# A linear-attention block with a gated FFN: one tile's mean on VectorE, one tile transposed by a DMA, and the last store from another queue

## The chip, the cores and the metric

The kernel runs on one core of a Trainium2 chip. The metric is the device time of one execution in microseconds; the kernel before has a median of 222.75 us over three runs (222.39 to 224.24).

## The reference

The input x has 2048 tokens of 640 features. All weights are bf16. Cut to what matters:

```python
xn = (x - mean(x)) / sqrt(var(x) + 1e-5)          # per token, no affine part
q, k, v = split(xn @ wqkv)                        # 32 heads of 20 features
phi = lambda t: where(t > 0, t + 1, exp(t)) + 1e-6
kv  = einsum("bhsd,bhse->bhde", phi(k), v)
z   = einsum("bhsd->bhd", phi(k))
o   = einsum("bhqd,bhde->bhqe", phi(q), kv) / (einsum("bhqd,bhd->bhq", phi(q), z) + 1e-6)
s   = o @ wo                                      # 640 to 640
g   = silu(relu(xn @ w1) @ w2)                    # FFN with 1728 inner features
out = x + s * g
```

## The kernel before

The tokens are 16 tiles of 128 and four chunks of 512. Every operation is put on an engine by hand, in the order in which the program text calls it; a small scheduler (`Sched`) finds the data dependences and adds the semaphore waits. So on each engine, and on each DMA queue, work runs strictly in the written order. Almost all DMAs are issued by SyncE's queue (SP); the first part of w1 is issued by ScalarE's.

The products with xn need it with features on partitions: `xnT`. Tiles 4 to 15 are normalised whole on VectorE (`LN_stats`: two statistics instructions, one aggregate, and 1/sqrt(var + eps) on GpSimd; then `LN_norm`) and transposed by a DMA from SP (`xnT_dma`, line 451). Tiles 0 to 3, which are needed first, are only centred (`center`, line 429) and their scale is applied later, when their keys and their gate are evicted. They are transposed by TensorE (`T_pe`, line 435, five 128 x 128 blocks) and copied out of PSUM by `T_copy` (lines 442 and 445). The mean of tiles 0 and 1 comes from `LN_stats` (lines 397 and 399); that of tiles 2 and 3 from an accumulating copy on ScalarE (`T_mean`, line 421).

While the inputs arrive, TensorE computes the first five of the 13 blocks of the FFN's inner features for chunk 0, one tile at a time: `H_first(t, fs, ks)` multiplies w1's blocks `fs`, contraction parts `ks`, with tile t (line 543, 128 columns each) into PSUM banks 2 to 6, and for tile 3 evicts each finished bank on ScalarE (`H_ev`, line 550). Bank 7 or 1 receives the transposes. The head of the program in its order:

```python
    H_first(0, (0, 1, 2), (0, 1)); H_first(0, (0, 1, 2), (2, 3, 4))   # two lines in the kernel
    LN_stats(1); center(1, 0, 2); T_pe(1, 0, 2, 7)
    ...
    H_first(0, (3, 4)); T_mean(3); center(2, 0, C)
    H_first(1, (0, 1)); T_pe(2, 0, C, 7); T_copy("ACT", 2, 0, C, 7); center(3, 0, C)
    H_first(1, (2, 3, 4)); T_pe(3, 0, C, 1); T_copy("ACT", 3, 0, C, 1)
    LN_stats(2); LN_stats(3)
    H_first(2); H_first(3, (4, 0, 1, 2, 3))
```

Then follow the keys of tiles 0 to 7 in turn with the rest of the FFN's blocks of chunk 0 (the list `order`): `K_step(t)` has the products of one tile's keys (`K_mm`, line 460, banks 0 and 1 or 6 and 7 by turns), the exponential on ScalarE (line 478 or 481), the rectified part (`K_relu`, line 487 on VectorE for tiles 0 and 1), and LayerNorm steps of tiles 4 to 7, whose transposes SP issues. The later chunks run queries (line 528) and FFN blocks by turns. After that come the sum over tokens of xn against phi(k) (line 786), the small products that make kv and kv times wo, the FFN's second half (line 841, `U_main`) with its silu on ScalarE, and the output products (line 887, `s_tile`): VectorE multiplies the gate in (line 909), adds x (line 894), and SP stores the tile (line 897). The last tile is cut in three parts (line 902): 320, 192 and 128 columns. GpSimd adds x to the first, VectorE to the other two together, and each of these two halves has its own store.

Of the kernel before, what the change touches and what calls it, by code (L numbers as in the profile page):

```python
# [4 lines left out]
ALU = mybir.AluOpType  # L5
ACTF = mybir.ActivationFunctionType
# [14 lines left out]
class Sched:  # L21
# [67 lines left out]

    def _hazards(self, R, W):  # L90
        agents = []
        for key in R:
            st = self.res.get(key)
# [29 lines left out]

    def op(self, E, fn, R=(), W=(), extra=()):
        return self.group(E, [fn], R, W, extra)
# [86 lines left out]
def bass_recurrent_scan__linear_attn_block__dense_activation_relu__prompt_kernel(  # L212
# [9 lines left out]
    Bb, S, D = A_x.shape  # L222
# [7 lines left out]
    C = D // P  # L230
# [3 lines left out]
    HN = D // 2  # L234
# [11 lines left out]
    out2 = out[0]  # L246
# [5 lines left out]
    xnT = reg1[:, :].rearrange("p (c s) -> p c s", c=C)  # L252
# [4 lines left out]
    xn = reg2[:, :].rearrange("p (t n) -> p t n", t=T)  # L257
# [6 lines left out]
    outb = reg3[:, VC * D:(VC + NOUT) * D].rearrange("p (a n) -> p a n", a=NOUT)  # L264
# [22 lines left out]
    xin = reg7[:, :].rearrange("p (t n) -> p t n", t=XR)  # L287
# [4 lines left out]
    ek = nc.alloc_sbuf_tensor("ek", [P, NEK, 2, D], bf)  # L292
# [27 lines left out]
    sc = Sched(nc, NDS)  # L320
    nds = [0]

    def dma(E, fn, R=(), W=(), extra=()):
        i = nds[0]
        nds[0] += 1
        return sc.dma(E, fn, i, R=R, W=W, extra=extra)

    def tok(t):
        return slice(P * t, P * (t + 1))
# [8 lines left out]
    def w_load(dst, src, key, extra=()):  # L338
# [9 lines left out]
          R=[("ident",)], W=[("ident",)])  # L348
# [16 lines left out]
    def w1_part(f):  # L365
# [6 lines left out]
        extra=[began])  # L372
# [21 lines left out]
    def LN_stats(t):  # L394
        xv = xin[:, t % XR, :]
        for a in range(2):
            sc.op("DVE", lambda eng, a=a: eng.bn_stats(stats[:, t, a, :], xv[:, HN * a:HN * (a + 1)]),  # L397
                  R=[("xin", t % XR)], W=[("stats", t, a)])
        sc.op("DVE", lambda eng: eng.bn_aggr(mv[:, t, :], stats[:, t, :, :].rearrange("p a b -> p (a b)")),
              R=[("stats", t, 0), ("stats", t, 1)], W=[("mv", t)])  # L400
        sc.op("POOL", lambda eng: eng.tensor_scalar(out=rsv[:, t:t + 1], in0=mv[:, t, 1:2], scalar1=EPS_LN,
                                                    scalar2=None, op0=ALU.add), R=[("mv", t)], W=[("rsv", t)])
        sc.op("POOL", lambda eng: eng.tensor_tensor(out=rsy[:, t:t + 1], in0=rsv[:, t:t + 1], in1=mhalf[:, :],
                                                    op=ALU.pow), R=[("rsv", t), ("mhalf",)], W=[("rsy", t)])
# [3 lines left out]
    def xnk(t, cs=range(C)):  # L408
        return [("xn", t, c) for c in cs]
# [7 lines left out]

    def T_mean(t):  # L420
        sc.op("ACT", lambda eng: eng.activation(out=ek[:, 0, 0, :], in_=xin[:, t, :], func=ACTF.Copy, scale=1.0 / D,
                                                accum_out=mean[:, t:t + 1]),
              R=[("xin", t)], W=[("mean", t), ("ek_e", 0)])

    sc.allow_unread.add(("ek_e", 0))

    def center(t, c0, c1):
        mk, m = (("mv", t), mv[:, t, 0:1]) if t < 2 else (("mean", t), mean[:, t:t + 1])
        return sc.op("DVE", lambda eng: eng.tensor_scalar(
            out=xn[:, t, P * c0:P * c1], in0=xin[:, t, P * c0:P * c1], scalar1=m, scalar2=None,  # L430
            op0=ALU.subtract), R=[("xin", t), mk], W=xnk(t, range(c0, c1)))

    def T_pe(t, c0, c1, b):
        psb = ps[b].bitcast(bf)
        sc.group("PE", [(lambda eng, c=c: eng.transpose(psb[:, P * c:P * (c + 1)], xn[:, t, P * c:P * (c + 1)], ident[:]))  # L435
                        for c in range(c0, c1)], R=xnk(t, range(c0, c1)) + [("ident",)], W=[("ps", b)])

    def T_copy(E, t, c0, c1, b):
        out = xnT[:, c0:c1, tok(t)]
        src = ps[b].bitcast(bf)[:, P * c0:P * c1].rearrange("p (c q) -> p c q", c=c1 - c0)  # L440
        if E == "ACT":
            sc.op("ACT", lambda eng: eng.activation(out=out, in_=src, func=ACTF.Copy), R=[("ps", b)],  # L442
                  W=xtk(t, range(c0, c1)))
        else:
            sc.op("DVE", lambda eng: eng.tensor_copy(out, src), R=[("ps", b)], W=xtk(t, range(c0, c1)))

    def xtk(t, cs=range(C)):
        return [("xnT", t, c) for c in cs]

    def xnT_dma(t):  # L450
        dma("SP", lambda eng: eng.dma_start_transpose(xnT[:, :, tok(t)], xn[:, t, :]), R=xnk(t), W=xtk(t))


    lastK = [None]
# [121 lines left out]
    def H_first(t, fs=range(5), ks=range(C)):  # L576
        for f in fs:
            H_mm(0, f, HF[f], P * t, P * t + P, ks)
            if t == 3:
                H_ev(0, f, HF[f])  # L580
# [10 lines left out]
    fill(1, 384)  # L591
    H_first(0, (0, 1, 2), (0, 1))
    H_first(0, (0, 1, 2), (2, 3, 4))
    LN_stats(1)
    center(1, 0, 2)
    T_pe(1, 0, 2, 7)
    held = center(1, 2, 5)
# [11 lines left out]
    H_first(0, (3, 4))  # L609
    T_mean(3)  # L610
    center(2, 0, C)
    H_first(1, (0, 1))
    T_pe(2, 0, C, 7)
    T_copy("ACT", 2, 0, C, 7)
    center(3, 0, C)
    H_first(1, (2, 3, 4))
    T_pe(3, 0, C, 1)
    T_copy("ACT", 3, 0, C, 1)
    LN_stats(2)
    LN_stats(3)  # L620
    H_first(2)
    H_first(3, (4, 0, 1, 2, 3))

    def z_split():
        sc.op("POOL", lambda eng: eng.tensor_copy(zhl[:, 0, :], zacc[:, :]), R=[("zacc",)], W=[("zhi",)])
        sc.op("POOL", lambda eng: eng.tensor_tensor(out=zhl[:, 1, :], in0=zacc[:, :], in1=zhl[:, 0, :], op=ALU.subtract),
# [54 lines left out]
            if t == 7:  # L681
                K_fin(t)

    order = [("K", 0), ("K", 1), 5, ("K", 2), 6, ("K", 3), 7, 8, ("K", 4), 9, ("K", 5), 10, ("K", 6), 11, ("K", 7), 12]
    for a in order:
        if isinstance(a, tuple):
            K_step(a[1])
        else:
            H_block(0, a, (2, 3, 4, 5)[(a - 5) % 4])
        if a == 6:  # L690
            LN_stats(6)
            K_fin(1)
            LN_norm(6)
            xnT_dma(6)
        if a == 8:
            LN_stats(7)
            K_fin(2)
            LN_norm(7)
            xnT_dma(7)
            K_fin(3)  # L700
# [4 lines left out]
    for j in range(1, J):  # L705
# [11 lines left out]
        for n, (kind, jj, f) in enumerate(blocks):  # L717
# [4 lines left out]
            if j + 1 < J:  # L722
# [6 lines left out]
                if n in (9, 12, 14, 17):  # L729
                    t = t0 + (9, 12, 14, 17).index(n)  # L730
# [27 lines left out]
    for a in range(2):  # L758
# [3 lines left out]
            W=[("w2", a)], extra=[lastX])  # L762
    for u in range(2):
        dma("SP", lambda eng, u=u: eng.dma_start(w2l[64 * u:64 * (u + 1), :], B_w2[NF * P:FF, :]),
            W=[("w2l", u)], extra=[lastX])
# [4 lines left out]
    for c in range(C):  # L770
        dma("SP", lambda eng, c=c: eng.dma_start(rep[:, c, :], rscr[P * c:P * (c + 1), :]),
            R=[("rscr", i) for i in range(J)], W=[("rep", c)], extra=[lastX])
# [61 lines left out]
    def bank(p, u):  # L834
        return 4 * ((p + 1) % 2) + 2 * u
# [43 lines left out]
    def s_tile(p, u, b, last=False):  # L879
        t = pairs[p][u]  # L880
        os_ = so[0] % NOUT
        so[0] += 1
        i = t // 4

        parts = [(b, 0, HN), (b + 1, HN, 512), (bank(7, 0), 512, D)] if last else [(b, 0, HN), (b + 1, HN, D)]
        for pb, lo, hi in parts:
            sc.group("PE", [(lambda eng, c=c, pb=pb, lo=lo, hi=hi: eng.matmul(  # L887
                ps[pb][:, 0:hi - lo], lhsT=pqT[:, c, tok(t)], rhs=wf[:, c, lo:hi],
                start=(c == 0), stop=(c == C - 1))) for c in range(C)],
                R=[("pqT", i, c) for c in range(C)] + wfk, W=[("ps", pb)])  # L890
        gk = [("g", t, 0), ("g", t, 1)]

        def add(E, lo, hi, keys):
            sc.op(E, lambda eng: eng.tensor_tensor(out=outb[:, os_, lo:hi], in0=tmpo[:, os_, lo:hi],  # L894
                                                   in1=xre[:, t, lo:hi], op=ALU.add),
                  R=[("tmpo", os_, k) for k in keys] + [("xre", t // 4)], W=[("outb", os_, k) for k in keys])
            dma("SP", lambda eng: eng.dma_start(out2[tok(t), lo:hi], outb[:, os_, lo:hi]),
                R=[("outb", os_, k) for k in keys])

        if last:  # L900
            for k, (pb, lo, hi) in enumerate(parts):
                sc.op("DVE", lambda eng, pb=pb, lo=lo, hi=hi: eng.tensor_tensor(  # L902
                    out=tmpo[:, os_, lo:hi], in0=ps[pb][:, 0:hi - lo], in1=g_sb[:, t, lo:hi], op=ALU.mult),
                    R=[("ps", pb)] + gk, W=[("tmpo", os_, k)])
                if k == 0:
                    add("POOL", lo, hi, (0,))
            add("DVE", HN, D, (1, 2))
        else:
            sc.op("DVE", lambda eng: eng.tensor_tensor(  # L909
                out=two(tmpo[:, os_, :]), in0=ps2(b, HN), in1=two(g_sb[:, t, :]), op=ALU.mult),  # L910
                R=[("ps", b), ("ps", b + 1)] + gk, W=[("tmpo", os_, k) for k in range(3)])
            add("DVE", 0, D, (0, 1, 2))
# [88 lines left out]
```

## Time and profile before

| | |
|---|---|
| median of three runs | 222.75 us (222.39 to 224.24) |
| profiled execution | 222.63 us, span 220.8 us |
| mean granted clock of TensorE | 0.998 |
| TensorE busy | 215.1 us of the span |
| VectorE, ScalarE, GpSimd busy | 113.4, 87.8, 43.8 us |
| DMA | 24.51 MB, mean 111 GB/s |

The span goes from the first to the last instruction that the profiler recorded. In a timeline row stand the start in us from the span's start, the duration, the engine (a q behind it is its sequencer, which issues DMAs), the line, the operation, the tile written and the tiles read by the program's names, shapes, and in brackets the idle time of the engine ahead of it and what ended it. `reg` is any of the large shared SBUF regions, `psT` is PSUM. Rows of one line that follow each other are merged and counted (x5). A DMA's landing is counted from its issue.

### The profile page before, as it was taken

To read this page: it belongs to the slowest core of one execution; us is meant where nothing else is said; L and a number is where in the kernel's file an instruction comes from. 1 tells how busy PE (TensorE), PEld (TensorE's weight loads), DVE (VectorE), ACT (ScalarE), POOL (GpSimd) and SP (SyncE) were. 2 spreads that over 40 slices of the span, in tenths; PEclk is the share of its full clock that TensorE was granted. 3 is DMA by queue.
4 is the path that set the end of the run, shared out by engine and by line. 5 is a ranking of instruction groups with operands and counts; after the bars stand their busy time and mean duration, and the time that the engine had idled before them with its cause. 6 is when DMAs were issued, how large, how long until landed. Compare 5 with 4: busy or idle time off the path is not lost.

```text
span 220.8 us, 3565 instructions
## 1 busy us (share of the span) xinstructions
PE 215.1 (97%) x1479; PEld 134.1 (61%) x1490; DVE 113.4 (51%) x193; ACT 87.8 (40%) x143; POOL 43.8 (20%) x66
## 2 busy tenths in 40 slices
PE   8899999999999999999999999999999999999994
PEld 2875554455545554444467778767767776776673
DVE  2848856789686999987700006603322222314063
ACT  3677775557656666555321114641021102110300
POOL 4232201269122997700000000000000000000001
PEclk9999999999999999999999999999999999999999
DMA  6994593213012105800069968378110100000002
GB/s 175 361 371 121 130 184 107 59 36 27 0 30 59 33 1 117 168 3 0 0 199 364 270 190 344 94 224 284 60 62 0 61 33 30 31 33 30 30 30 88
DMA packets 28812, 24.51 MB, mean 111 GB/s; under 512 B 11812, under 2 KB 28156, under 8 KB 28796
## 3 DMA queue, kind: packets, MB, share of 16 engines
q1 hardware_dynamic: 28140, 23.79, 37.3%
q10 hardware_dynamic: 656, 0.49, 0.9%
q8 instruction: 11, 0.18, 0.3%
q14 instruction: 5, 0.04, 0.1%
HBM read 15.75 MB, written 5.24 MB: 95 GB/s over the span
## 4 chain that ended last, share of the span: by engine, by line
PE 95%; DMA 2%; DVE 1%; issue 0%; SPq 0%
PE psT L841 26%; PE psT L543 25%; PE psT L786 10%; PE psT L460 10%; PE psT L528 10%; PE psT L887 10%; DMA reg<-in_A_x_dram 2%; PE psT L857 1%; PE psT L565 1%; PE psT L797 1%; PE psT L808 1%; PE psT L644 1%; PE psT L435 1%; DVE reg L902 0%; DVE stats L397 0%
## 5 line engine op out<-in xcount | busy, mean ns | idle before, releaser
L543 PE MATMUL psT<-reg 128*128 128x512 bf16 (+1 forms) x326 | 60.1, 330 | 1.3 <-DMA reg<-in_B_w_dram 0.7
L841 PE MATMUL psT<-reg,hT 128*128 128x320 bf16 x416 | 60.1, 299 | 0.0
L841 PEld LDWEIGHTS psT<-reg,hT 128*128 128x128 bf16 x416 | 40.4, 98 | 16.4 <-issue 1.1
L543 PEld LDWEIGHTS psT<-reg 128*128 128x128 bf16 x335 | 28.5, 98 | 26.6 <-ACT reg L442 1.0
L909 DVE TENSOR_TENSOR reg<-psT,reg 128x640 bf16<-128x640 f32 x15 | 12.4, 825 | 54.0 <-PE psT L887 54.0
L550 ACT ACTIVATE hT<-psT 128x512 bf16<-128x512 f32 x52 | 30.7, 599 | 16.1 <-PE psT L543 16.0
L875 ACT ACTIVATE reg<-psT 128x640 bf16<-128x640 f32 (+1 forms) x13 | 8.4, 661 | 44.3 <-PE psT L841 24.9
L894 POOL TENSOR_TENSOR reg<-reg 128x320 bf16<-128x320 bf16 x1 | 0.8, 787 | 124.6 <-DVE reg L902 124.6
L528 PE MATMUL psT<-reg 128*128 128x512 bf16 x98 | 24.4, 379 | 0.1
L460 PE MATMUL psT<-reg 128*128 128x320 bf16 x160 | 24.2, 299 | 0.0
L469 POOL TENSOR_TENSOR zacc<-zacc,reg 128x640 f32<-128x640 f32 x16 | 23.8, 1484 | 1.9 <-DVE reg L503 1.0
L887 PE MATMUL psT<-reg,pqT 128*128 128x320 bf16 (+2 forms) x165 | 24.0, 295 | 0.0
L786 PE MATMUL psT<-reg 128*128 128x320 bf16 x160 | 21.9, 299 | 0.0
L460 PEld LDWEIGHTS psT<-reg 128*128 128x128 bf16 x160 | 15.5, 98 | 8.3 <-ACT ek L481 0.3
L887 PEld LDWEIGHTS psT<-reg,pqT 128*128 128x128 bf16 x165 | 15.9, 98 | 6.0
L786 PEld LDWEIGHTS psT<-reg 128*128 128x128 bf16 x160 | 15.7, 98 | 6.2
L538 DVE SCALAR_TENSOR_TENSOR pqT<-er 128x512 bf16<-128x512 bf16 x20 | 17.1, 854 | 0.7
L528 PEld LDWEIGHTS psT<-reg 128*128 128x128 bf16 x100 | 9.7, 98 | 11.7 <-DVE er L536 0.6
L397 DVE BATCH_NORM_STATS2 stats<-reg 128x6 f32<-128x320 bf16 x32 | 14.0, 480 | 5.0 <-DMA reg<-in_A_x_dram 5.0
L535 ACT ACTIVATE er<-psT 128x512 bf16<-128x512 f32 x20 | 12.0, 598 | 8.9 <-PE psT L528 8.1
L536 DVE TENSOR_SCALAR er<-psT 128x512 bf16<-128x512 f32 x20 | 13.6, 679 | 3.0 <-ACT er L535 3.0
L503 DVE TENSOR_TENSOR reg<-ek 128x640 bf16<-128x640 bf16 x16 | 13.5, 844 | 1.5 <-ACT ek L494 1.0
(62 smaller groups left out, 133.3 us busy)
## 6 DMA issues: line engine op xcount, KB each, us to landing
reg<-in_A_x_dram SPq DMA_DIRECT2D x16, 160.0 KB, 3.5
rscr<-rden SPq DMA_DIRECT2D x4, 640.0 KB, 10.8
reg<-rscr SPq DMA_DIRECT2D x5, 512.0 KB, 6.2
reg<-in_A_x_dram SPq DMA_DIRECT2D x4, 640.0 KB, 6.9
out_dram<-reg SPq DMA_DIRECT2D x15, 160.0 KB, 1.8
reg<-in_A_wqkv_dram SPq DMA_DIRECT2D x2, 800.0 KB, 6.7
reg<-in_B_w_dram SPq DMA_DIRECT2D x1, 1120.0 KB, 5.6
reg<-in_B_w_dram SPq DMA_DIRECT2D x1, 960.0 KB, 9.3
```

The source lines that it names most:

```text
L397: sc.op("DVE", lambda eng, a=a: eng.bn_stats(stats[:, t, a, :], xv[:, HN * a:HN * (a + 1)]), R=[("xin", t % XR)], W=[("stats", t, a)])
L460: fns.append(lambda eng, a=a, k=k: eng.matmul(ps[b + a][:, 0:HN], lhsT=xnT[:, k, tok(t)], rhs=wqk[:, k, D + HN * a:D + HN * (a + 1)], star ...
L469: sc.op("POOL", lambda eng: eng.tensor_tensor(out=zacc[:, :], in0=zacc[:, :], in1=pk[:, t, :], op=ALU.add), R=[("zacc",), ("pk", t)], W=[( ...
L503: sc.op("DVE", lambda eng: eng.tensor_tensor(out=pk[:, t, :], in0=e_, in1=r_, op=ALU.add), R=[("ek_e", es), ("ek_r", es)], W=[("pk", t)])
L528: sc.group("PE", [(lambda eng, k=k: eng.matmul(ps[b], lhsT=wqk[:, k, P * f:P * (f + 1)], rhs=rhs(k), start=(k == 0), stop=(k == C - 1))) f ...
L536: sc.op("DVE", lambda eng: eng.tensor_scalar(out=r_, in0=ps[b], scalar1=0.0, scalar2=1e-6, op0=ALU.max, op1=ALU.add), R=[("ps", b), ("er_e ...
L538: sc.op("DVE", lambda eng: eng.scalar_tensor_tensor(out=pqT[:, f, schunk(j)], in0=e_, scalar=1.0, in1=r_, op0=ALU.min, op1=ALU.add), R=[(" ...
L543: return sc.group("PE", [(lambda eng, k=k: eng.matmul(ps[b][:, lo:hi], lhsT=w1_sb[:, k, P * f:P * (f + 1)], rhs=xnT[:, k, 512 * j + lo:512 ...
L550: sc.op("ACT", lambda eng: eng.activation(out=hT[:, f, schunk(j)], in_=ps[b], func=ACTF.Relu), R=[("ps", b)], W=[("hT", j, f)])
L786: fns.append(lambda eng, t=t, a=a: eng.matmul(ps[b + a][:, 0:HN], lhsT=xn[:, t, P * k:P * (k + 1)], rhs=pk[:, t, HN * a:HN * (a + 1)], sta ...
L841: sc.group("PE", [(lambda eng, f=f, n=n: eng.matmul(ps[b + n][:, 0:HN], lhsT=hT[:, f, tok(t)], rhs=w2_sb[:, f, HN * n:HN * (n + 1)], start ...
L887: sc.group("PE", [(lambda eng, c=c, pb=pb, lo=lo, hi=hi: eng.matmul(ps[pb][:, 0:hi - lo], lhsT=pqT[:, c, tok(t)], rhs=wf[:, c, lo:hi], sta ...
```

## The change

Four edits. The mean of tile 1 is made by one VectorE tensor_scalar with an accumulated output, and `LN_stats(1)`, still needed for the variance, moves behind tile 3's DMA. Tile 3 is transposed by a DMA that ScalarE's queue issues, instead of by TensorE and a ScalarE copy; every later `xnT_dma` on SP waits until it has landed (`extra=first_T`). In TensorE's order six of tile 1's products move ahead of tile 2's transposes, and all of tile 3's blocks move behind the keys of tile 0. In the last tile the parts become 256, 192 and 192 columns; GpSimd adds the first 256, VectorE the other 384, and that second store is issued by ScalarE's queue.

```diff
+    def T_mean(t, E="ACT"):
+        if E == "ACT":
...
+        else:
+            sc.op("DVE", lambda eng: eng.tensor_scalar(out=ek[:, 1, 0, :], in0=xin[:, t, :], scalar1=1.0 / D, scalar2=0.0,
+                                                       op0=ALU.mult, op1=ALU.add, accum_out=mean[:, t:t + 1]),
+                  R=[("xin", t)], W=[("mean", t), ("ek_e", 1)])
...
-        mk, m = (("mv", t), mv[:, t, 0:1]) if t < 2 else (("mean", t), mean[:, t:t + 1])
+        mk, m = (("mv", t), mv[:, t, 0:1]) if t < 1 else (("mean", t), mean[:, t:t + 1])
...
-    def xnT_dma(t):
-        dma("SP", lambda eng: eng.dma_start_transpose(xnT[:, :, tok(t)], xn[:, t, :]), R=xnk(t), W=xtk(t))
+    first_T = []
+
+    def xnT_dma(t, E="SP"):
+        d = dma(E, lambda eng: eng.dma_start_transpose(xnT[:, :, tok(t)], xn[:, t, :]), R=xnk(t), W=xtk(t), extra=first_T)
+        if E != "SP":
+            first_T.append(d)
...
-    LN_stats(1)
+    T_mean(1, "DVE")
     center(1, 0, 2)
...
     center(2, 0, C)
-    H_first(1, (0, 1))
+    H_first(1, (0, 1, 2, 3, 4), (0, 1))
+    H_first(1, (0, 1), (2, 3, 4))
     T_pe(2, 0, C, 7)
     T_copy("ACT", 2, 0, C, 7)
     center(3, 0, C)
-    H_first(1, (2, 3, 4))
-    T_pe(3, 0, C, 1)
-    T_copy("ACT", 3, 0, C, 1)
+    H_first(1, (2, 3, 4), (2, 3, 4))
+    xnT_dma(3, "ACT")
+    LN_stats(1)
     LN_stats(2)
     LN_stats(3)
     H_first(2)
-    H_first(3, (4, 0, 1, 2, 3))
...
-    order = [("K", 0), ("K", 1), 5, ...]
+    order = [("K", 0), None, ("K", 1), 5, ...]        # None: H_first(3, (4, 0, 1, 2, 3))
...
-        parts = [(b, 0, HN), (b + 1, HN, 512), (bank(7, 0), 512, D)] if last else [(b, 0, HN), (b + 1, HN, D)]
+        parts = [(b, 0, 256), (b + 1, 256, 448), (bank(7, 0), 448, D)] if last else [(b, 0, HN), (b + 1, HN, D)]
...
-            add("DVE", HN, D, (1, 2))
+            add("DVE", 256, D, (1, 2), "ACT")
```

More of the change, by code (lines that the diff above doesn't have):

```diff
@@ L416, in LN_norm @@
             x_load(t + XR)
[L420 to L425, printed above, removed]
+    def T_mean(t, E="ACT"):
+        if E == "ACT":
+            sc.op("ACT", lambda eng: eng.activation(out=ek[:, 0, 0, :], in_=xin[:, t, :], func=ACTF.Copy, scale=1.0 / D,
+                                                    accum_out=mean[:, t:t + 1]),
+                  R=[("xin", t)], W=[("mean", t), ("ek_e", 0)])
+        else:
+            sc.op("DVE", lambda eng: eng.tensor_scalar(out=ek[:, 1, 0, :], in0=xin[:, t, :], scalar1=1.0 / D, scalar2=0.0,
+                                                       op0=ALU.mult, op1=ALU.add, accum_out=mean[:, t:t + 1]),
+                  R=[("xin", t)], W=[("mean", t), ("ek_e", 1)])
+    sc.allow_unread.update([("ek_e", 0), ("ek_e", 1)])
     def center(t, c0, c1):
-        mk, m = (("mv", t), mv[:, t, 0:1]) if t < 2 else (("mean", t), mean[:, t:t + 1])
+        mk, m = (("mv", t), mv[:, t, 0:1]) if t < 1 else (("mean", t), mean[:, t:t + 1])
         return sc.op("DVE", lambda eng: eng.tensor_scalar(
@@ L682, in K_step @@
                 K_fin(t)
-    order = [("K", 0), ("K", 1), 5, ("K", 2), 6, ("K", 3), 7, 8, ("K", 4), 9, ("K", 5), 10, ("K", 6), 11, ("K", 7), 12]
+    order = [("K", 0), None, ("K", 1), 5, ("K", 2), 6, ("K", 3), 7, 8, ("K", 4), 9, ("K", 5), 10, ("K", 6), 11, ("K", 7), 12]
     for a in order:
-        if isinstance(a, tuple):
+        if a is None:
+            H_first(3, (4, 0, 1, 2, 3))
+        elif isinstance(a, tuple):
             K_step(a[1])
@@ L891, in s_tile, with add @@
         gk = [("g", t, 0), ("g", t, 1)]
-        def add(E, lo, hi, keys):
+        def add(E, lo, hi, keys, Q="SP"):
             sc.op(E, lambda eng: eng.tensor_tensor(out=outb[:, os_, lo:hi], in0=tmpo[:, os_, lo:hi],
@@ L896, in add @@
                   R=[("tmpo", os_, k) for k in keys] + [("xre", t // 4)], W=[("outb", os_, k) for k in keys])
-            dma("SP", lambda eng: eng.dma_start(out2[tok(t), lo:hi], outb[:, os_, lo:hi]),
+            dma(Q, lambda eng: eng.dma_start(out2[tok(t), lo:hi], outb[:, os_, lo:hi]),
                 R=[("outb", os_, k) for k in keys])
```

## The prediction

> **What bounds the kernel now.** I read the parts of the page first: busy time, slices, and the chain that ended last.
>
> ```profile
> span 220.8 us, 3565 instructions
> PE 215.1 (97%) x1479; PEld 134.1 (61%) x1490; DVE 113.4 (51%) x193; ACT 87.8 (40%) x143; POOL 43.8 (20%) x66
> PE 95%; DMA 2%; DVE 1%; issue 0%; SPq 0%
> ```
>
> TensorE is busy for 97% of the span and carries 95% of the chain. The chain in order of time shows it without a gap from the second transposes to the last output product; the two rows at its end are VectorE's. Only the first 7 us and the last 4 us can be shortened by waiting less. In between, five transposes are all that the change takes off TensorE, so what matters is whether a new wait opens in the head. Next I read the head engine by engine in the timeline (start, duration, engine, line, tiles, count, what ended the idle time).
>
> ```profile
> 6.06 1.00 PE L543 MATMUL psT<-reg 128*128 128x128 bf16 x15 [0.72 <-DMA reg<-in_B_w_dram]
> 7.21 0.57 PE L435 MATMUL psT<-ident,reg 128*128 128x128 bf16 x5 [0.15 <-DVE reg L429]
> 7.62 1.35 PE L543 MATMUL psT<-reg 128*128 128x128 bf16 x20
> 8.81 0.44 PE L435 MATMUL psT<-ident,reg 128*128 128x128 bf16 x5
> 9.09 1.00 PE L543 MATMUL psT<-reg 128*128 128x128 bf16 x15
> 9.93 0.44 PE L435 MATMUL psT<-ident,reg 128*128 128x128 bf16 x5
> 10.20 2.96 PE L543 MATMUL psT<-reg 128*128 128x128 bf16 x50
> 13.00 2.88 PE L460 MATMUL psT<-reg 128*128 128x320 bf16 x20
> ```
>
> These rows are tile 0's blocks, tile 1's transposes, then by turns blocks and the transposes of tiles 2 and 3; from 10.20 the blocks of tiles 2 and 3, 50 products in 2.80 us, so 56 ns each; at 13.00 the keys of tiles 0 and 1. The chain gives those 20 key products 2.72 us, 1.36 per tile, so the keys are through at 15.72. This is my checkpoint: behind it the order on TensorE is the old one.
>
> ```profile
> 13.16 2.72 PE psT L460 x20
> ```
>
> **Part 1: tile 1's mean by accumulation.** Removed ahead of the centring are two statistics and one aggregate; added is one 640-wide tensor_scalar with an accumulated output, from the same arrival at 5.71.
>
> ```profile
> 5.71 0.89 DVE L397 BATCH_NORM_STATS2 stats<-reg 128x6 f32<-128x320 bf16 x2 [0.92 <-DMA reg<-in_A_x_dram]
> 6.63 0.21 DVE L399 BATCH_NORM_AGGREGATE mv<-stats 128x2 f32<-128x12 f32 x1
> 6.87 0.52 DVE L429 TENSOR_SCALAR reg<-reg,mv 128x256 bf16<-128x256 bf16 x2
> 8.10 0.38 DVE L429 TENSOR_SCALAR reg<-reg,mean 128x640 bf16<-128x640 bf16 x1
> 8.53 0.18 ACT L421 ACTIVATION_READ_ACCUMULATOR ek<-reg 128x1 f32 x1
> 15.38 0.89 DVE L487 TENSOR_SCALAR ek<-psT,rsy 128x640 bf16<-128x640 f32 x1 [2.08 <-ACT ek L478]
> 2.25 0.43 SPq L339 DMA_DIRECT2D reg<-in_B_w_dram  x1
> reg<-in_B_w_dram SPq DMA_DIRECT2D x1, 320.0 KB, 5.1
> ```
>
> No row shows a VectorE accumulation. Its bounds are a 640-wide tensor_scalar from SBUF (0.38) and one from PSUM (0.89), with up to 0.18 for reading the sum as ScalarE does. The mean is then ready between 6.09 and 6.78 instead of 6.84, and the centring starts 0.1 to 0.75 us earlier. TensorE cannot use that: its 15 products end at 6.06 + 15 x 0.056 = 6.90, so the transposes come at most 0.31 earlier, and behind them stand blocks 3 and 4 of tile 0, which need the second part of w1: issued 2.25, landed 5.1 later, at 7.35. With the tenth of a microsecond from a landing to its product they start at 7.45 instead of 7.62. The gain is 0.17 at most, 0 at least; I take 0.17. Tile 1's statistics, moved behind tile 3's centring, are wanted by its exponential at 16: five microseconds of cover.
>
> **Part 2: tile 3 off TensorE, and the new order.** From 7.45 TensorE has 26 products (10 of tile 0, 16 of tile 1) ahead of tile 2's transposes, which so start at 7.45 + 1.46 = 8.91, against 8.81. What follows waits for the copy out of PSUM.
>
> ```profile
> 9.29 0.70 ACT L442 ACTIVATE reg<-psT 128x640 bf16<-128x640 bf16 x1 [0.57 <-PE psT L435]
> 8.75 0.39 DVE L429 TENSOR_SCALAR reg<-reg,mean 128x640 bf16<-128x640 bf16 x1 [0.28 <-ACT ek L421]
> 12.08 2.56 ACT L550 ACTIVATE hT<-psT 128x512 bf16<-128x512 f32 x5 [0.97 <-PE psT L543]
> 14.55 0.79 ACT L478 ACTIVATE ek<-psT,rsy 128x640 bf16<-128x640 f32 x1
> ```
>
> In the old order copy 2 ends at 9.99, 1.18 after the first of its transposes, and 15 products and tile 3's five transposes (0.28) cover it up to 10.20. In the new order only nine products stand there (0.50): TensorE is free at 8.91 + 0.28 + 0.50 = 9.69, the copy is there at 8.91 + 1.18 = 10.09, and tile 2's blocks start at 10.12. So the five transposes saved turn into 0.43 of idling, and of all that only 0.08 is left. Then 25 products (1.40) and tile 0's keys (1.36) end at 12.88. The key weights are there in time, at 4.82 + 5.2 = 10.02:
>
> ```profile
> 4.82 0.38 SPq L339 DMA_DIRECT2D reg<-in_A_wqkv_dram  x1
> DMA to landing us min/median/max: 5.2/5.2/5.2
> ```
>
> **The transfer decides.** At 12.88 TensorE wants tile 3. ScalarE's queue issues it behind copy 2, which starts at 8.91 + 0.48 = 9.39; tile 3's centring is done by 9.14. The issue is at 9.4 if the queue runs ahead of the engine, at 10.1 if it waits for the copy. The issue holds ScalarE's queue for about 1.3 us, as it holds SP's; behind it stands the exponential of tile 0, not wanted before 12.9.
>
> ```profile
> 17.02 1.32 SPq L451 DMA_TRANSPOSE reg<-reg  x1
> DMA to landing us min/median/max: 2.6/2.6/3.9
> 10.00:11.00 1.00, 1.00 (x22) 1.00 (x20) 0.96 (x4) 0.60 (x1) 0.65 (x2) 1.00 1.07 379
> reg<-in_B_w_dram ACTq DMA_DIRECT2D x1, 480.0 KB, 4.8
> ```
>
> The second row is the landing time of the twelve transposes of line 451 (least, median, most); the window row shows the DMA engines full (last two columns: share, GB/s) just when tile 3 would fly. Its price lies between 2.6, the quiet one, and 4.8, the only load of ScalarE's queue beside SP's, which was three times as large. I take 3.9, the worst of the twelve: it is nearest in kind. Landing is then at 13.3 (ends: 12.0, and 10.1 + 4.8 = 14.9). Tile 3's blocks start at 13.4, end at 14.8, and tile 1's keys at 16.16: **0.44 later** than 15.72, if nothing else opens.
>
> The Trainium skill, "VectorE: DVE Perf Modes", section The three transpose paths, lists 390 ns for a 128 x 128 block on TensorE and 1309 ns by DMA. Five such blocks in a row would make 6.5 us, a landing at 15.9 and a time near 225.5 by my sum (an estimate); the trace, with five blocks landed in 2.6, does not bear that out.
>
> If the transfer is in time, another wait is next: tile 1's keys need bank 6, emptied by ScalarE only behind the exponential of tile 0. That one starts some 0.2 after the keys, at 13.07 (0.79), the eviction (0.60 for one, five in 2.56) ends near 14.4, and TensorE would be there at 12.88 + 1.40 = 14.28. So the keys end at 15.8 at the earliest: the head gains nothing even then (+0.1).
>
> SP's transposes of tiles 4 to 7 now wait for tile 3's landing. Tile 4's was issued at 17.02 and becomes possible near 15.5, after the landing: no cost, unless tile 3 is very late. The x loads behind it on SP then wait too, with eight tiles already there.
>
> **Part 3: the end.**
>
> ```profile
> L902 DVE TENSOR_TENSOR reg<-psT,reg 128x320 bf16<-128x320 f32 x1 | 0.5, 492 | 1.1 <-PE psT L887 1.1
> L902 DVE TENSOR_TENSOR reg<-psT,reg 128x192 bf16<-128x192 f32 x1 | 0.4, 359 | 0.0
> L902 DVE TENSOR_TENSOR reg<-psT,reg 128x128 bf16<-128x128 f32 x1 | 0.3, 292 | 0.0
> 217.41 0.79 POOL L894 TENSOR_TENSOR reg<-reg 128x320 bf16<-128x320 bf16 x1 [124.63 <-DVE reg L902]
> 217.85 0.52 DVE L894 TENSOR_TENSOR reg<-reg 128x320 bf16<-128x320 bf16 x1
> L894 DVE TENSOR_TENSOR reg<-reg 128x640 bf16<-128x640 bf16 x1 | 0.5, 491 | 0.0
> 218.22 0.33 SPq L897 DMA_DIRECT2D out_dram<-reg  x1
> 218.60 0.43 SPq L897 DMA_DIRECT2D out_dram<-reg  x1
> ```
>
> The last product ends when it did. Its multiply is 192 wide, not 128: +0.07, so the add starts at 217.92. The old add took 0.52 for 320 columns beside GpSimd's, while 640 columns alone took 0.49: the two slowed each other. Now GpSimd has 256 columns and starts some 0.2 earlier, ending near 217.85 (0.79 x 256/320 = 0.63, an estimate), so the 384-wide add runs alone. Bounds 0.29 (0.49 x 384/640) and 0.52; I take 0.40, the middle, end 218.32. The old store waited 0.2 for SP to issue the one before; ScalarE's queue is free, so it issues at 218.35 instead of 218.60. Gain **0.25** (0.13 to 0.36), with the same landing time.
>
> **Sum.** 222.63 for the profiled execution (span 220.8 and 1.8 around it), + 0.44 - 0.25 = 222.82. The median of the runs, 222.75, lies 0.12 above that execution: 222.9. One for one, the time is that of before if tile 3 lands near 13.1.
>
> **Rivals.**
>
> *Late transfer, slower.* The DMA engines serve ScalarE's queue by turns beside SP's deep queue, and small pieces lose against long rows: tile 3 lands only when SP's backlog thins. For it speaks the full window above; against it, that the 480 KB beside x loads landed in 4.8. If it lands with the last x tile, 16.5, tile 3's blocks start at 16.6, the keys end at 19.4, +3.6 - 0.25: 226.1. From 13.1 on this decides the sign, from 15.3 it exceeds 1%.
>
> The Trainium skill, "DMA: Bandwidth & Descriptors", section SWDGE vs HWDGE vs iDMA, says that each DMA engine has 16 queues and goes round them, switching at packets. No row here shows a transpose in such company, so that its turn is short is a possibility only.
>
> *Transfer in time, a little faster.* Landing by 12.9, as the quiet 2.6 gives from either issue: +0.1 - 0.27, 222.6 with the 0.12. The full window speaks against it.
>
> *The queue does not run ahead.* Issue at 10.1, landing 14.0 with my 3.9: 222.9 + 0.7 = 223.6. SP shows no case with work of its own ahead of an issue, so this stays open.
>
> *The mean does not come earlier* because the accumulation costs its upper bound: 0.17 lost at most, 223.1; w1's landing hides the rest.
>
> **How the numbers follow.** Forecast 0.42 (with the mean's rival, which moves it by too little to part), in time 0.25, queue waits 0.18, late 0.15. The last reaches from 224.6 to 227. The range is 222.1 to 224.9: the low end is the best of the second case less the spread between runs, the high end takes the bound 14.9 and leaves about a tenth above. Over 1%, 2.2 us, is about what a measurement of this kernel can tell from no change. No case gains that, since head and tail do not hold it: faster 0.02. Two thirds of the late case lose it, and a little of the queue's: slower 0.11. Within: 0.87.
>
> **What would show it.** Right: blocks of tile 0 at 7.45 after w1's landing; a TensorE wait of 0.4 on the copy at line 442 before tile 2's blocks; a wait on the DMA of tile 3 at about 12.9 of 0.1 to 1 us; keys done 0.2 to 1 later; the last store issued before 218.5 less that shift. Wrong: no wait on tile 3, or one over 2 us; a later wait on tiles 4 to 7 (the last of them landed 0.1 before its keys: 26.01 + 3.9 against 30.06); a gain from anything in between.
>
> ```profile
> 26.01 1.21 SPq L451 DMA_TRANSPOSE reg<-reg  x1
> 30.06 1.52 PE L460 MATMUL psT<-reg 128*128 128x320 bf16 x10
> ```

## The result and the profile after

The changed kernel takes 229.64 us (median of six runs, 228.85 to 230.23), the kernel before 222.57 (six runs). The ratio is 1.0321, 95% interval 1.0295 to 1.0347: 7 us slower. The prediction had 222.9, with 224.9 as its upper end. The profiled execution took 229.01 us with a span of 227.3, 6.5 more than before; in it and in the one of 228.85 TensorE's mean granted clock is 0.990 and 0.992, in the four slower ones 0.983 to 0.985.

The parts of the page:

```profile
span 227.3 us, 3567 instructions
PE 91%; DMA 6%; SPq 1%; DVE 1%; ACT 0%; issue 0%; ACTq 0%
```

The chain around the place where the time went (start, duration, what the chain runs through):

```profile
9.13 8.97 DMA reg<-reg
...
18.15 2.85 PE psT L553 x25
21.00 1.69 PE psT L470 x10
22.69 1.08 PE psT L553 x5
```

The DMA share of the chain went from 2% to 6%. One row explains that: tile 3's transfer, issued at 9.13, landed 8.97 us later. The rows below it hold a second loss. Counted from start to start in the timeline below, tile 3's 25 products take 2.64 us (18.15 to 20.79), where 25 such products needed 1.40 before, and tile 1's keys 1.73 (20.79 to 22.52) instead of 1.36. (The chain counts to the end of the last product, about 0.2 behind the start of the next.)

TensorE in the timeline of the changed kernel (L440 are the transposes, L553 the FFN's blocks, L470 the keys; in brackets the idle time and what ended it):

```profile
5.84 1.00 PE L553 MATMUL psT<-reg 128*128 128x128 bf16 x15 [0.43 <-ACT reg L447]
...
7.18 1.63 PE L553 MATMUL psT<-reg 128*128 128x128 bf16 x26
8.65 0.44 PE L440 MATMUL psT<-ident,reg 128*128 128x128 bf16 x5
8.93 0.67 PE L553 MATMUL psT<-reg 128*128 128x128 bf16 x9
9.89 1.57 PE L553 MATMUL psT<-reg 128*128 128x128 bf16 x25 [0.29 <-ACT reg L447]
11.29 1.52 PE L470 MATMUL psT<-reg 128*128 128x320 bf16 x10
18.15 2.85 PE L553 MATMUL psT<-reg 128*128 128x128 bf16 x25 [5.34 <-DMA reg<-reg]
20.79 1.90 PE L470 MATMUL psT<-reg 128*128 128x320 bf16 x10
22.52 1.24 PE L553 MATMUL psT<-reg 128*128 128x512 bf16 x5
```

TensorE could have started tile 3 at 12.65 (11.29 and 1.36 for the keys) and started at 18.15, 5.50 later; the row's 5.34 counts from the end of the last key product. The windows behind the wait show why the products then are slow (the number behind the five engines is the clock that TensorE was granted, 1.00 being full speed; the last two are DMA share and GB/s):

```profile
18.00:20.00 2.00, 1.85 (x18) 1.85 (x19) 0.00 (x0) 1.10 (x3) 0.00 (x0) 0.53 0.97 284
20.00:22.60 2.60, 2.60 (x21) 2.01 (x19) 0.00 (x0) 1.63 (x4) 0.00 (x0) 0.70 0.19 22
```

The profiler's clock records put it at half from 18.12 to 21.53, for 3.41 us. In the chain tile 1's keys end at 22.69 instead of 15.88, 6.81 later. From start to start that is 5.50 of waiting, 1.24 + 0.37 of slow clock and 0.46 of waiting for the copy (9.43, when nine products behind 8.93 are through, to 9.89), less 0.28 for the five transposes, 0.28 for the mean (measured below) and 0.22 for a first block that starts at 5.84 instead of 6.06: 6.79. The end then gives 0.3 back.

The end of the changed kernel:

```profile
222.75 1.53 PE L898 MATMUL psT<-reg,pqT 128*128 128x256 bf16 x15
224.00 0.67 POOL L905 TENSOR_TENSOR reg<-reg 128x256 bf16<-128x256 bf16 x1 [124.43 <-DVE reg L913]
224.72 0.36 DVE L905 TENSOR_TENSOR reg<-reg 128x384 bf16<-128x384 bf16 x1
225.11 0.38 ACTq L908 DMA_DIRECT2D out_dram<-reg  x1
```

The last product ends at 224.28, the span 3.0 later; before, it was 3.3.

### The profile page after: what moved, and what is told of

Read it like the earlier page. It is cut to its first block, busy times and chain, and to the rows that moved or that the text cites. A ratio compares the mean times of both kernels' runs of the same rounds, so it can differ in the third digit from the quotient of the medians.

```text
span 227.3 us, 3567 instructions
## 1 busy us (share of the span) xinstructions
PE 217.3 (96%) x1485; PEld 135.3 (60%) x1485; DVE 114.2 (50%) x195; ACT 87.4 (38%) x142; POOL 43.6 (19%) x66
## 4 chain that ended last, share of the span: by engine, by line
PE 91%; DMA 6%; SPq 1%; DVE 1%; ACT 0%; issue 0%; ACTq 0%
PE psT L852 25%; PE psT L553 24%; PE psT L898 10%; PE psT L797 10%; PE psT L538 10%; PE psT L470 9%; DMA reg<-reg 4%; DMA reg<-in_A_x_dram 2%; PE psT L868 1%; PE psT L575 1%; PE psT L808 1%; PE psT L819 1%; SPq L336 1%; PE psT L653 1%; ACT ek L422 0%
## 5 line engine op out<-in xcount | busy, mean ns | idle before, releaser
L553 PE MATMUL psT<-reg 128*128 128x512 bf16 (+1 forms) x335 | 63.3, 338 | 6.1 <-DMA reg<-reg 5.3
L553 PEld LDWEIGHTS psT<-reg 128*128 128x128 bf16 x335 | 29.7, 101 | 32.6 <-DMA reg<-reg 5.7
L538 PE MATMUL psT<-reg 128*128 128x512 bf16 x100 | 24.9, 379 | 0.0
L470 PE MATMUL psT<-reg 128*128 128x320 bf16 x160 | 24.7, 302 | 0.0
L905 POOL TENSOR_TENSOR reg<-reg 128x256 bf16<-128x256 bf16 x1 | 0.7, 668 | 124.4 <-DVE reg L913 124.4
L797 PE MATMUL psT<-reg 128*128 128x320 bf16 x160 | 21.9, 299 | 0.0
L470 PEld LDWEIGHTS psT<-reg 128*128 128x128 bf16 x160 | 15.8, 99 | 8.4
L797 PEld LDWEIGHTS psT<-reg 128*128 128x128 bf16 x160 | 15.7, 98 | 6.2
L538 PEld LDWEIGHTS psT<-reg 128*128 128x128 bf16 x100 | 9.7, 98 | 11.6 <-DVE er L546 0.6
L513 DVE TENSOR_TENSOR reg<-ek 128x640 bf16<-128x640 bf16 x16 | 13.5, 843 | 1.9 <-ACT hT L560 0.8
```

The lines of the kernel that those rows point to most:

```text
L470: fns.append(lambda eng, a=a, k=k: eng.matmul(ps[b + a][:, 0:HN], lhsT=xnT[:, k, tok(t)], rhs=wqk[:, k, D + HN * a:D + HN * (a + 1)], star ...
L513: sc.op("DVE", lambda eng: eng.tensor_tensor(out=pk[:, t, :], in0=e_, in1=r_, op=ALU.add), R=[("ek_e", es), ("ek_r", es)], W=[("pk", t)])
L538: sc.group("PE", [(lambda eng, k=k: eng.matmul(ps[b], lhsT=wqk[:, k, P * f:P * (f + 1)], rhs=rhs(k), start=(k == 0), stop=(k == C - 1))) f ...
L553: return sc.group("PE", [(lambda eng, k=k: eng.matmul(ps[b][:, lo:hi], lhsT=w1_sb[:, k, P * f:P * (f + 1)], rhs=xnT[:, k, 512 * j + lo:512 ...
L797: fns.append(lambda eng, t=t, a=a: eng.matmul(ps[b + a][:, 0:HN], lhsT=xn[:, t, P * k:P * (k + 1)], rhs=pk[:, t, HN * a:HN * (a + 1)], sta ...
```

## The experiments

The theory after this profile: tile 3's transfer is the whole loss, late because of SP's loads, and the slow clock is its consequence. Rivals: the reordered program or one of the other edits costs something too; the transposing or ScalarE's queue is slow by itself.

### One edit at a time

**undo_T**: the changed kernel with tile 3 back on TensorE.

```diff
-    H_first(1, (0, 1, 2, 3, 4), (0, 1)); H_first(1, (0, 1), (2, 3, 4))
+    H_first(1, (0, 1))
...
-    H_first(1, (2, 3, 4), (2, 3, 4)); xnT_dma(3, "ACT")
+    H_first(1, (2, 3, 4)); T_pe(3, 0, C, 1); T_copy("ACT", 3, 0, C, 1)
...
+    H_first(3, (4, 0, 1, 2, 3))
...
-    order = [("K", 0), None, ("K", 1), 5, ...]
+    order = [("K", 0), ("K", 1), 5, ...]
```

> Tile 3 goes back to TensorE and a ScalarE copy, in the old order of TensorE; the accumulated mean and the new last tile stay. Theory (tile 3's transfer is the whole loss): the wait of 5.3 us, and the slow clock behind it, are gone; the head ends 0.1 to 0.2 earlier than in the kernel before and the tail 0.3, so 0.998 of before, 222.1 to 222.4. Rival (the mean on VectorE or the moved statistics cost something too): 1.000 or above.

Measured: 221.84 us, ratio 0.9988 (0.9972 to 1.0004). The 7 us are gone; the other edits do no harm that the runs could show. Whether this version is faster than the kernel before is not decided by the interval, though its profile shows both gains: 6.64 us from the first block to the keys (5.99 to 12.63; before 6.94), and 3.0 from the last product's end to the span's (217.1 to 220.1; before 3.3).

**mean_only**: undo_T with the old last tile and store, so the accumulated mean alone.

```diff
-        parts = [(b, 0, 256), (b + 1, 256, 448), (bank(7, 0), 448, D)] if last else ...
+        parts = [(b, 0, HN), (b + 1, HN, 512), (bank(7, 0), 512, D)] if last else ...
...
-            add("DVE", 256, D, (1, 2), "ACT")
+            add("DVE", HN, D, (1, 2))
```

> Only the mean of tile 1 on VectorE, with tile 1's statistics behind tile 3's centring. Prediction's step: the transposes come early, but blocks 3 and 4 of tile 0 wait for w1's second part; 0 to 0.2 us gained at the keys, ratio 0.999 to 1.000. Rival (the moved statistics delay tile 4's): ratio above 1.001 with a wait of the keys of tiles 4 to 7.

Measured: 222.19 us, ratio 0.9994 (0.9981 to 1.0006). Its TensorE rows:

```profile
5.95 1.00 PE L553 MATMUL psT<-reg 128*128 128x128 bf16 x15 [0.58 <-DMA reg<-in_B_w_dram]
6.79 0.44 PE L440 MATMUL psT<-ident,reg 128*128 128x128 bf16 x5
7.29 1.29 PE L553 MATMUL psT<-reg 128*128 128x128 bf16 x20
...
12.61 2.88 PE L470 MATMUL psT<-reg 128*128 128x320 bf16 x20
```

From the first block to the keys it takes 6.66 us; before it was 6.94 (6.06 to 13.00). So the mean brings 0.28. The gap between the transposes, through at 7.07, and the next block at 7.29 is the wait for w1's second part, as predicted: issued at 2.24, it landed 5.0 later. No verdict can show a gain of this size: the first loads land at slightly different times from run to run, and the first block starts at 5.84 to 6.06 in the three profiles quoted so far.

**tail_only**: the kernel before with the new last tile and store.

> Only the new cut of the last tile and its store from ScalarE's queue, on the kernel before. By the profile after, the time from the last product's end to the last landing shrinks from 2.8 to 2.5: 0.3 less, ratio 0.9986. Rival (an average of runs hides it): the interval of the ratio holds 1, but the profile still shows the last store issued right behind VectorE's add.

Measured: 222.15 us, ratio 0.9995 (0.9978 to 1.0012). The rival's reading holds: the runs do not decide it, and the profile shows the mechanism, one add of 384 columns alone on VectorE and the store issued behind it:

```profile
218.37 0.36 DVE L894 TENSOR_TENSOR reg<-reg 128x384 bf16<-128x384 bf16 x1
218.76 0.36 ACTq L897 DMA_DIRECT2D out_dram<-reg  x1
```

### Is it the transfer's company?

**T_on_SP**: tile 3's transpose issued by SP, ahead of the loads.

```diff
-    w1_load(2, [held]); x_load(4); x_load(5); w1_load(3); x_load(6); x_load(7); w_load(wqk[:, :, 0:D], ...)
...
-    xnT_dma(3, "ACT")
+    xnT_dma(3, "SP")
+    w1_load(2, [held]); x_load(4); x_load(5); w1_load(3); x_load(6); x_load(7); w_load(wqk[:, :, 0:D], ...)
```

> Tile 3's transpose issued by SP, ahead of the loads of w1's third and fourth part, x tiles 4 to 7 and the query weights, which so start some 3.5 us later; all else as in the changed kernel. Theory (the transfer was late because of the loads issued ahead of it and beside it): it lands 2.6 to 3.0 after its issue near 9.0, by 12, TensorE does not wait for it at 12.7, the clock stays full; whole 222.2 to 223.2, depending on whether w1's third part is in time for block 5. Rival (the reordered program itself is slow, whatever the transfer does): 226 or more.

Measured: 223.16 us, ratio 1.004 (1.0022 to 1.0058). The transfer, then TensorE:

```profile
L459 SPq DMA_TRANSPOSE reg<-reg x1: 1325/1325/1325, 8.8 to 8.8; - x1
DMA to landing us min/median/max: 2.7/2.7/2.7
```

```profile
12.65 1.56 PE L553 MATMUL psT<-reg 128*128 128x128 bf16 x25
...
17.46 1.53 PE L470 MATMUL psT<-reg 128*128 128x320 bf16 x10 [0.66 <-DVE ek L497]
```

It lands in 2.7, TensorE does not wait for it, and the reordered program by itself is not what cost 7 us. But the delayed loads make a new wait: tile 2's keys wait 0.66 for VectorE's rectified part of tile 0, which stands on VectorE behind tile 4's statistics, and these start at 15.53 instead of 12.44, because x tile 4 now arrives some 3 us later. Even with the transfer in time, this order gains nothing.

**hold_all**: the transfer stays on ScalarE's queue, and SP's loads are issued when it has landed.

```diff
-    w1_load(2, [held]); x_load(4); x_load(5); w1_load(3); x_load(6); x_load(7); w_load(wqk[:, :, 0:D], ...)
...
     xnT_dma(3, "ACT")
+    w1_load(2, first_T); x_load(4); x_load(5); w1_load(3); x_load(6); x_load(7); w_load(wqk[:, :, 0:D], ...)
```

> As the changed kernel, but w1's third part and everything behind it is issued only when tile 3 has landed; beside the transfer only the key weights' last piece is under way. Theory (SP's loads delay it): lands 2.6 to 3.0 after issue, near 12, no wait for tile 3, full clock; then w1's third part is late for block 5 and x tile 4 for its statistics: 222.5 to 224.5. Rival (ScalarE's queue is slow for transposes): lands at 15 or later though alone.

Measured: 226.77 us, ratio 1.0175 (1.0131 to 1.0218): slower, though the interval leaves open whether by 2%, and more than expected. The landing came 4.3 after the issue, between the theory's 2.6 to 3.0 and the rival's 6. TensorE waited for it, for w1's third part, and for VectorE; the transfer, then TensorE:

```profile
L459 ACTq DMA_TRANSPOSE reg<-reg x1: 1282/1282/1282, 9.1 to 9.1; - x1
DMA to landing us min/median/max: 4.3/4.3/4.3
```

```profile
13.41 1.57 PE L553 MATMUL psT<-reg 128*128 128x128 bf16 x25 [0.67 <-DMA reg<-reg]
...
17.93 1.02 PE L553 MATMUL psT<-reg 128*128 128x512 bf16 x4 [1.60 <-DMA reg<-in_B_w_dram]
19.97 2.85 PE L470 MATMUL psT<-reg 128*128 128x320 bf16 x10 [1.02 <-DVE ek L497]
```

Without company the 9 us shrink to 4.3. Why not to 2.6 is taken up under **fetch_hold_all**.

**plain_copy**: undo_T, and at the transfer's place ScalarE's queue issues a plain copy of the same tile in the same 640 pieces of 256 bytes.

```diff
     T_pe(3, 0, C, 1)
...
+    dma("ACT", lambda eng: eng.dma_start(pqT[:, :, 0:P], xn[:, 3, :].rearrange("p (c n) -> p c n", c=C)), ...)
     T_copy("ACT", 3, 0, C, 1)
```

> Tile 3 back on TensorE; at the place of its transfer ScalarE's queue issues a plain copy of the same tile, 640 pieces of 256 bytes, into a buffer that nobody reads then. Theory 1 (the queue and the company make it late, not the transposing): it lands 8 to 9 us after its issue. Theory 2 (the transposing does): it lands in 3 to 5. In both nobody waits: 222 to 223.

Measured, in a single run: 221.92 us. Nobody waits, and the copy lands as late as the transpose:

```profile
L629 ACTq DMA_DIRECT2D pqT<-reg x1: 680/680/680, 9.1 to 9.1; - x1
DMA to landing us min/median/max: 8.9/8.9/8.9
```

Theory 2 falls: in this place a plain copy is as late, so the place in time and on the queue is enough. It does not show that the transposing costs nothing, for the two get to their 9 us by different ways, as the next counts show.

### Where the nine microseconds go

The traces hold every DMA packet. Counted per half microsecond, SP's queue / ScalarE's queue:

```
start     10.0   10.5   11.0   11.5   12.0   12.5   13.0    13.5    14.0    14.5    15.0    15.5    16.0    16.5    17.0
after     184/0  181/0  168/0  168/0  162/0  167/0  156/42  128/128 53/50   2/2     3/3     101/101 127/126 127/129 132/91
plain     189/0  186/0  167/0  156/0  160/0  161/0  153/44  132/121 121/122 125/126 119/117 119/95  133/20  141/6   137/5
hold_all  0/126  0/424  0/120  0/0    0/2    0/0
```

Alone, the first piece moves 1.2 us after the issue (9.06 to 10.30). In the changed kernel it moves 4.0 after (9.13 to 13.16); until then the engines carry SP's loads only. From there both queues move packet for packet, 127 to 126, although SP's packets are then of 1152 or 1280 bytes and tile 3's of 256. And from 14.5 to 15.5 both stand nearly still. The plain copy waits as long for its first piece and does not stand still: 625 of its 656 packets have moved by 16.0, but the last 31 take until 17.3. That it lands as late as the transpose is in part chance. The Trainium skill, "DMA: Bandwidth & Descriptors", section SWDGE vs HWDGE vs iDMA, says that an engine goes round its queues and switches at packets: the second phase agrees with it, the first is not in it. The size of the packets tells the loads apart, and so where tile 3 stood: in the changed kernel its first piece moves when 472 of the 640 packets of w1's fourth part (issued at 8.13) are out, and 0.4 ahead of the first of x tile 6, which SP had issued at 8.62. So the second queue started its transfer 4.0 after the issue, where SP's own loads of that moment took 3.4 (w1's fourth part, first piece at 11.53) and 4.9 (x tile 6, 13.52).

**hold_behind**: only w1's fourth part and what follows is held until tile 3 has landed; w1's third part and x tiles 4 and 5 stay ahead of it.

```diff
-    w1_load(3); x_load(6); x_load(7); w_load(wqk[:, :, 0:D], ...)
...
     xnT_dma(3, "ACT")
+    w1_load(3, first_T); x_load(6); x_load(7); w_load(wqk[:, :, 0:D], ...)
```

> As the changed kernel, but w1's fourth part, x tiles 6 and 7 and the query weights are issued only when tile 3 has landed; w1's third part and x tiles 4 and 5 are still issued ahead of it. Theory 1 (the transfer starts only when what was issued ahead has gone out, about 12.8, then shares with what is beside it): it starts at 12 to 12.9, is alone then, and lands near 14. Theory 2 (it starts at once and takes turns with whatever is there): its packets start at 10.3 beside the loads ahead and it lands at 12.5 to 13.7. Rival (a transpose from ScalarE's queue takes 9 us in any company): 18.

Measured, in a single run: 225.9 us. The first piece moved at 11.37, 2.2 after the issue, between the two theories; the landing came at 14.9, after 5.7; the transfer, then TensorE's wait:

```profile
L459 ACTq DMA_TRANSPOSE reg<-reg x1: 1282/1282/1282, 9.2 to 9.2; - x1
DMA to landing us min/median/max: 5.7/5.7/5.7
```

```profile
14.97 1.68 PE L553 MATMUL psT<-reg 128*128 128x128 bf16 x25 [2.09 <-DMA reg<-reg]
```

All but two of its packets had moved by 13.0. A packet of 16 KB on another queue, 12.7 to 13.9, fell into this transfer as well (see **fetch_hold_all**), so not all of the 5.7 is due to the loads.

**behind_T**: the same loads are issued a few tenths behind the transfer, not held for its landing.

```diff
+            if a == 0: late[0] = o           # the first statistics instruction of LN_stats(t)
...
     xnT_dma(3, "ACT"); LN_stats(1)
+    w1_load(3, [late[0]]); x_load(6); x_load(7); w_load(wqk[:, :, 0:D], ...)
```

> As the changed kernel, but w1's fourth part and the loads after it are issued a few tenths of a microsecond behind tile 3's transfer instead of ahead of it (they wait for the first statistics of tile 1, about 9.4), and not for its landing. Theory 1 (a transfer on the other queue starts when the loads issued ahead of it are nearly out; those issued behind it only share): its packets start near 11.4, as where those loads were held back, then go one for one with the load's; landing near 15 to 16, TensorE's wait 2 to 3 instead of 5.3, whole 226 to 228. Theory 2 (the length of the whole backlog decides): start near 13.2 and landing near 18 as in the changed kernel.

Measured: 229.47 us, ratio 1.0328 (1.0308 to 1.0349): nothing gained. The first piece moved at 12.17, 3.2 after the issue, again between the theories, and the landing was as late as ever:

```profile
L463 ACTq DMA_TRANSPOSE reg<-reg x1: 1290/1290/1290, 9.0 to 9.0; - x1
DMA to landing us min/median/max: 8.9/8.9/8.9
```

So loads issued ahead delay the start, loads issued just behind still delay it, and those in flight beside it slow the rest. A strict order of issue does not explain these starts: in **behind_T** w1's fourth part, issued 0.2 behind the transfer, moves its first piece at 11.45, ahead of the transfer's. The runs do not say which stage holds the pieces back.

**fetch_after** and **fetch_hold_all**: a 16 KB packet of the queue that the page calls instruction falls into the transfer, at 13.7 in the changed kernel and at 11.4 in **hold_all**; it takes about 1 us. The warm-up (products of constants at the start, whose results nobody reads) is cut finer and gets more instructions, so that this fetch of instructions comes earlier.

```diff
-    fill(9)
+    def narrow(eng):
+        eng.wait_ge(done_sems["POOL"], 1); eng.wait_ge(done_sems["POOL"], 1)
+        return eng.matmul(ps[0][:, 0:P], lhsT=cones, rhs=cwide[:, 0:P], start=True, stop=True)
+    sc.group("PE", [narrow] * 36, W=[("ps", 0)])
```

> The same warm-up on the kernel that holds SP's loads until tile 3 has landed. There the fetch stood at 11.36 and the transfer, alone from 10.3, landed at 13.4, 4.3 after its issue. Theory (the fetch): with it out of the way the landing is 2.6 to 2.9 after the issue, near 12. Rival (ScalarE's queue needs 4.3 for a transpose): 13.4 again.

Measured, in a single run: 225.54 us. The fetch moved to 8.8, the landing came 2.6 after the issue:

```profile
L459 ACTq DMA_TRANSPOSE reg<-reg x1: 1283/1283/1283, 9.7 to 9.7; - x1
DMA to landing us min/median/max: 2.6/2.6/2.6
```

> As the changed kernel, but TensorE's first nine warm-up products of 512 columns are 36 of 128 columns, each behind two waits that are already met: the same work and about 130 more instructions in TensorE's stream, so the 16 KB instruction fetch that falls into tile 3's transfer at 13.7 comes some microseconds earlier. Theory (the 1.5 us in which all transfers stand still, 14.0 to 15.5, come from the fetch holding one DMA engine while the transpose runs over all of them): no standstill, landing near 16.5 instead of 18.1, 1 to 1.6 us faster than the changed kernel. Rival (the standstill belongs to transpose and loads in each other's company): landing at 18 again.

Measured: 229.29 us, ratio 1.032 (1.0294 to 1.0346). The fetch moved to 11.1, ahead of the first piece, but the landing came 8.4 after the issue instead of 9.0, and the warm-up itself made the issue half a microsecond later. Data rates by window, the changed kernel first, then fetch_after, then plain_copy (last column):

```profile
14.00:15.00 1.00, 0.00 (x0) 0.00 (x0) 1.00 (x2) 0.00 (x0) 0.53 (x1) 1.00 1.96 74
```

```profile
14.00:15.00 1.00, 0.00 (x0) 0.00 (x0) 0.96 (x4) 0.18 (x1) 0.22 (x1) 1.00 1.50 186
```

```profile
14.00:15.00 1.00, 1.00 (x9) 0.73 (x8) 0.03 (x1) 0.94 (x2) 0.18 (x1) 1.00 1.08 342
```

The fetch explains the landing of the lone transfer (4.3 against 2.6); **T_on_SP** agrees, where a fetch at 11.2 came just behind the last piece (11.0) and the landing took 2.7. In company it explains only part of the standstill: without it the rate still fell to 186 GB/s, while the plain copy, with a fetch at 13.5 beside it, kept 342. The theory fails for the changed kernel: the standstill was there with the transpose beside the loads and not with the copy, and it was deeper where the fetch fell into it. How the two hold each other up is not shown.

### The slow clock

**warm**: the changed kernel with 23 products of constants into the free bank 7 during the wait.

```diff
...
         if a is None:
+            fill(23, b=7)
             H_first(3, (4, 0, 1, 2, 3))
```

> As the changed kernel, with 23 products of constants into bank 7 between tile 0's keys and tile 3's blocks: 4.9 us of work that nothing uses, inside the wait. Theory (the idling lowered TensorE's granted clock to half for 3.4 us, which cost 1.8 of the 7 us): the clock stays at 1, tile 3's blocks take 1.4 again, 227.7 to 228.0. Rival (the slow 25 products have another cause, such as late weights): 229.5 as before.

Measured: 227.63 us, ratio 1.0234 (1.0202 to 1.0266), about 2 us less than the changed kernel; TensorE, then the window of 18 to 20 us:

```profile
12.80 4.98 PE L355 MATMUL psT<-const-bfloat16-1.0 128*128 128x512 bf16 x22
17.79 1.57 PE L553 MATMUL psT<-reg 128*128 128x128 bf16 x25
19.20 1.52 PE L470 MATMUL psT<-reg 128*128 128x320 bf16 x10
```

```profile
18.00:20.00 2.00, 2.00 (x31) 1.78 (x29) 0.00 (x0) 1.72 (x4) 0.00 (x0) 1.00 1.13 259
```

The granted clock stays at 1 and the blocks start every 56 ns again (25 from 17.79 to 19.20). In this run the transfer also landed 0.4 earlier (17.74), so the clock's own share is about 1.6, as much as the 1.24 + 0.37 read from the changed kernel's timeline.

## Why the prediction was wrong

**The step that failed is the transfer's price.** The prediction knew that it decides, and put it between 2.6 and 4.8, taking 3.9. It was 9.0. The value came from transposes behind SP's own loads, after the head's backlog or near its end, and the upper bound from the early load of w1, which met only SP's first few loads. No row of before showed a transfer entering on the second queue against a full one, so 4.8 was no bound. The nearest rows were SP's own loads of that moment, and they took longer: w1's fourth part, issued at 8.88, landed after 5.9, and the query weights (800 KB), issued at 10.41, after 8.2.

```profile
L339 SPq DMA_DIRECT2D reg<-in_A_wqkv_dram x1: 441/441/441, 10.4 to 10.4; - x1
DMA to landing us min/median/max: 8.2/8.2/8.2
```

The rival of the late transfer had the direction and a part of the mechanism, the backlog and the packets taking turns; the 4.0 us before the first piece and the standstill were not in it. It had a landing at 16.5, where 18.1 was measured, and a chance of 0.15.

**A term was missing**: the clock. The price of late landing was put at one for one. A wait of 5.5 us cost 7.1, because TensorE's clock was halved for 3.4 us behind it. With both, the prediction's own sum comes out: 222.63 with the landing at 18.1 gives + 5.2 - 0.25, and 1.6 for the clock, 229.2, against 229.0 for the profiled execution.

**The steps that held.** Blocks 3 and 4 of tile 0 wait for w1's second part. The wait for copy 2, caused by the cover that tile 3's transposes had been, is there: 0.46 from start to start (0.29 in the row, which counts from the end of the last product), predicted 0.43. TensorE was ready for tile 3 at 12.65, predicted 12.88. ScalarE's queue does run ahead of its engine: the issue and copy 2 both start at 9.13, so that rival is out.

```profile
9.13 0.70 ACT L447 ACTIVATE reg<-psT 128x640 bf16<-128x640 bf16 x1 [0.60 <-PE psT L440]
9.13 1.35 ACTq L459 DMA_TRANSPOSE reg<-reg  x1
```

**Smaller sizes.** The accumulation took 0.82, near the bound of 0.89, and the reading of the sum (0.08) ended with it; and yet the mean gained 0.28, above the 0.17 allowed: w1's second part arrived a tenth earlier than in the profile before, and the first block also moves by that much between runs.

```profile
5.26 0.82 DVE L426 TENSOR_SCALAR_CACHE_REDUCE ek<-reg 128x640 bf16<-128x640 bf16 x1 [0.40 <-DMA reg<-in_A_x_dram]
6.00 0.08 DVE L426 DVE_READ_ACCUMULATOR ek<-reg 128x1 f32 x1
```

The end gained 0.3 (predicted 0.25): GpSimd's add ended at 224.67, before VectorE's began at 224.72, and that one took 0.36.

**The feared waits on tiles 4 to 7** did not come on their own: their transposes were issued later, but so was everything on TensorE.

## What to carry to other kernels

Here a transfer that entered on a second queue while the first held microseconds of loads did not pass them: price it by what the first queue's own loads of that moment take to land, not by its own quiet landing time, or issue it ahead of the loads and ask which of those is then late. When a step leaves an engine, the work that it covered is uncovered too; here five transposes saved turned into a wait for a copy. And a wait of some microseconds on TensorE can cost more than itself; here cheap products in the gap kept the clock.

## What the runs showed of the hardware that was not expected

Four things. A 160 KB transfer from ScalarE's queue, transposing or plain, landed 8.4 to 9.0 us after its issue beside a full SP queue (five runs), and a transpose 2.6 alone; the first piece waited up to 4.0 us, and then packets went one for one, 256 bytes against 1152 or 1280. With a transpose together with loads all transfers came nearly to a stop for about a microsecond (74 GB/s between 14 and 15 us), with the plain copy they did not. A 16 KB instruction fetch made a lone transpose land at 4.3 instead of 2.6. And a shorter gap is enough to lose the clock: in **hold_behind**, a wait of 2.09 us was followed by this window:

```profile
16.30:19.60 3.30, 3.08 (x16) 1.82 (x15) 0.00 (x0) 1.96 (x5) 0.00 (x0) 0.50 0.96 317
```

The Trainium skill, "TensorE: Matmul & The Clock Gate", section Why this matters for your kernels, warns of gaps above about 3 us; here 2.1 were followed by half the clock, while the kernel before, with gaps of up to 0.7, kept it.

It is not the length of one gap that decides in these traces. The clock records come in steps of 3.41 us, at a phase that differs from run to run: half clock from 18.12 to 21.53 in the changed kernel, 16.29 to 19.70 in **hold_behind**, 19.93 to 23.34 in **hold_all**, and for two steps, 15.55 to 22.37, in **behind_T**. In the twelve profiled executions that have such records, the clock was at half in just those steps that followed a step in which TensorE was busy for at most 41% of the time; after 44% and more it stayed full. The wait of 2.09 left 39% of its step busy. **fetch_hold_all**, with gaps of 0.57 and 1.02 in one step, still had 54% and kept the clock. So the same wait can cost different amounts, by where the steps fall.
